# Strassen's seven products for the second matrix of a mixture-of-experts layer, one product after the other, with a transposed result

## The chip, the core and the metric

The kernel runs on one core of one Trainium2 chip. The metric is the device time of one execution in microseconds. The core has a matrix engine (TensorE, PE in the profile; its weight loads are PEld), a vector engine (VectorE, DVE), a scalar engine (ScalarE, ACT), GpSimd (POOL) and a queue (SyncE, SP) from which every DMA of this kernel is issued. Matmuls write into PSUM, which has eight banks of 128 partitions x 512 fp32 columns.

## The reference

Attention without a softmax feeds two MLPs ("MoE" layers with one expert) in a row, all in fp32. 4608 tokens, model width 512, hidden width 2048:

```python
kv = np.einsum('bhsd,bhse->bhde', k, v)
out = np.einsum('bhsd,bhde->bhse', q, kv)
x = out / np.sqrt(np.mean(out * out, axis=-1, keepdims=True) + 1e-06) * g_norm
...
h = x @ w_in                       # first MoE
g = s * np.maximum(h, 0.0) ** 2 + b
x = g @ w_out
h = x @ w_in2                      # second MoE
g = h * (1.0 / (1.0 + np.exp(-1.702 * h)))
return g @ w_out2
```

The weights arrive as 64-bit numbers, seen in the kernel as pairs of 32-bit words.

## The kernel before, in words

**Precision.** Every fp32 operand is split into a high part (rounded to the matmul's float32r) and a low part (the rest). One product of two 128-wide pieces is three matmuls: high x high, high x low, low x high. ScalarE makes high parts (a copy), VectorE low parts (a subtraction).

**Tiling.** The tokens are nine blocks of 512 (`T`), the hidden width 16 tiles of 128 (`NF`), the model width four tiles of 128 (`NP`). Activations are kept transposed (features on partitions, tokens on columns). A first product of a block (`mlp_h`, line 405) is 12 matmuls of 512 columns per hidden tile, a second product (`mlp_o`, 443) 12 matmuls per hidden tile into four PSUM banks that are accumulated over all 16 hidden tiles. In the first MoE the weights of the second product are the stationary operand and the result stays transposed; in the second MoE the activations are stationary, and the result comes out with tokens on partitions, as the output wants it.

**Plain blocks and pairs.** Three blocks of the first MoE (`NPLAIN`) and the last block of the second run plainly (`plain`, 599). All others run as pairs of blocks (`strassen`, 615): three pairs in the first MoE, four in the second. In a pair the first product is done by Strassen's method in Winograd's form: with the operands cut into quarters, seven products (`PRODUCTS`, line 41) take the place of eight. `g1_product` (484) does one of the seven for two hidden tiles, 6 matmuls; `g1_sum` (518) adds the seven results into the four quarters, on VectorE out of PSUM; product 4 adds onto product 0's bank, product 6 onto product 3's. `g1_act` (542) applies the activation. The second product of a pair is the ordinary one: for each hidden tile f and each of the two blocks, 12 matmuls (`mlp_o`), whose operands `g2_hi` (565) and `g2_lo` (569) prepare from the activated tile `R[f]`, and whose weights `wo_load` (179) reads back from DRAM, 512 KB each.

**Operands.** The seven operands of the token side (`x_operands`, 640, with `x_load`, `x_sub`, `x_hi`, `x_lo`) are made during the second product of the pair before, those of the weight side are made once (`s_sums`, `op_hi`, `op_lo`, `op_store`, 198 to 226), kept in DRAM (`wsd`) and loaded for each pair (`op_load`, 233). The second MoE's weights are prepared while the first MoE's pairs run (the loop at 751): those of the first product as eight operands, those of the second as a high and a low half (`w_hi`, 159; `w_lo`, 163; `wo_store`, 173).

**Order.** Nothing is scheduled by a planner: every step is entered with a slot by `at(slot, function, ...)` (581), the entries are sorted by slot, and the instructions are emitted in that order. Each engine and the SP queue run their instructions in this order, and waits come from the data and the buffers. A slot is 12 matmuls of 512 columns; a pair's first stage has 28 slots (half a slot per product), its second stage 32. A load is entered `LEAD` = 4 slots ahead of its use, `g2_hi` 2.5 and `g2_lo` 2.0 slots ahead:

```python
at(base + 2 * f - LEAD, wo_load, m, f)
...
slot = base + 2 * f + n
at(slot, mlp_o, m, j + n, f)
...
at(slot - 2.5, g2_hi, m, j + n, f, n)
at(slot - 2.0, g2_lo, m, j + n, f, n)
```

SBUF buffers are 42 large ones (two tiles of 512 columns, `new4`) and 22 small ones (`new2`), reused in the order in which they were given back; so are the eight PSUM banks. The attention of later blocks (`attention`, 595) runs as small units within the first stages of the first MoE's first two pairs: a product, a square on ScalarE, a high and low part, two matmuls for the mean (`att_mean`, 335), then a root and a correction.

Of the kernel before, what the change touches and what calls it, by code (L numbers as in the profile page):

```python
# [60 lines left out]
def kernel(ctx: ExitStack, tc: tile.TileContext, qT, kv_h, kvt, cst,  # L61
# [111 lines left out]
    def wo_store(m, f):  # L173
        w = W[m, f, 1]
        nc.sync.dma_start(out=wod[m][f], in_=w.bitcast(F32))
        if m:
            drop(W.pop((m, f, 1)))

    def wo_load(m, f):
        w = W[m, f, 1] = new4(F32R, "w")  # L180
        nc.sync.dma_start(out=w.bitcast(F32), in_=wod[m][f])

    def a_store(f):
        w = W[0, f, 0]
        for c, name in enumerate((("A11", "A12"), ("A21", "A22"))[f % 2]):
            nc.sync.dma_start(
                out=wsd[0][f // 2][:, OPS.index(name), :].rearrange("p (h c) -> p h c", h=2),
                in_=w[:, :, c * 256:(c + 1) * 256].bitcast(F32),
            )
# [8 lines left out]
    def s_sums(m, i):  # L198
        a, a2 = (vals[m, 2 * i + n, 0].bitcast(F32) for n in range(2))
        s12, s34 = sums[m, i] = new2(F32, "s12"), new2(F32, "s34")  # L200
        lo, hi = slice(0, 256), slice(256, 512)
        dve.tensor_add(out=s12[:, lo], in0=a2[:, lo], in1=a2[:, hi])
        dve.tensor_sub(out=s34[:, lo], in0=a[:, lo], in1=a2[:, lo])
        dve.tensor_sub(out=s12[:, hi], in0=s12[:, lo], in1=a[:, lo])
        dve.tensor_sub(out=s34[:, hi], in0=a[:, hi], in1=s12[:, hi])

    def op_source(m, i, k):
        return vals[m, 2 * i + k, 0] if k < 2 else sums[m, i][k - 2]

    def op_hi(m, i, k):  # L210
        src = op_source(m, i, k).bitcast(F32)
        t = parts[m, i, k] = new4(F32R, "op")
        act.activation(t[:, :, 0:256], src.rearrange("p (a c) -> p a c", a=2), AF.Copy)

    def op_lo(m, i, k):
        src = op_source(m, i, k)
        t = parts[m, i, k]
# [4 lines left out]
    def op_store(m, i, k):  # L222
        t = parts.pop((m, i, k))
        for a, name in enumerate((("A11", "A12"), ("A21", "A22"), ("S1", "S2"), ("S3", "S4"))[k]):
            nc.sync.dma_start(out=wsd[m][i][:, OPS.index(name), :], in_=t[:, a, :].bitcast(F32))
        drop(t)

    def op_done(m, i):
        drop(*sums.pop((m, i)), *(vals.pop((m, 2 * i + n, 0)) for n in range(2)))
# [8 lines left out]
    def wi_load(m, f):  # L238
        t = W[m, f, 0] = new4(F32R, "w")
        for a, name in enumerate((("A11", "A12"), ("A21", "A22"))[f % 2]):  # L240
            nc.sync.dma_start(out=t[:, a, :].bitcast(F32), in_=wsd[m][f // 2][:, OPS.index(name), :])

    def wi_part(m, f, h, c):
        w = W[m, f, 0]
# [160 lines left out]
    def mlp_h(m, j, f):  # L405
# [3 lines left out]
        for c in range(NP):  # L409
            wh, wlo = (wi_part(m, f, i, c) for i in range(2))  # L410
# [32 lines left out]
    def mlp_o(m, j, f):  # L443
        gh, gl = G.pop((m, j, f))
        w = W[m, f, 1]
        wh, wlo = w[:, 0, :], w[:, 1, :]
        if f == 0:
            acc[m, j] = [psum("o") for c in range(NP)]
        for c in range(NP):
            o = acc[m, j][c]  # L450
            cc = slice(c * P, (c + 1) * P)
# [4 lines left out]
            for n, (a, x) in enumerate(pairs):  # L456
                pe.matmul(o, lhsT=a, rhs=x, start=(f == 0 and n == 0), stop=(f == NF - 1 and n == 2))  # L457
# [5 lines left out]
    def mlp_store(m, j):  # L463
# [9 lines left out]
        for c, t in enumerate(staged):  # L473
            if m == 0:
                nc.sync.dma_start(out=xd[1][j][c], in_=t)
                done.add((1, j, c))
            else:
                nc.sync.dma_start(out=out[j * T + c * P:j * T + (c + 1) * P, :], in_=t)
            drop(t)
# [4 lines left out]
    def g1_product(m, i, k):  # L484
# [5 lines left out]
        if first:  # L490
            st[k] = psum("abcdefg"[k])
        else:
            st[k] = st[0] if k == 4 else st[3]
# [14 lines left out]
    def relu2(m, r, src=None):  # L508
        if m == 0:
            act.activation(r, r if src is None else src, AF.Relu)  # L510
        else:
            src = r if src is None else src
            t = new2(F32, "t")
            act.activation(t, src, AF.Sigmoid, scale=1.702)
            dve.tensor_mul(out=r, in0=src, in1=t)
            drop(t)

    def g1_sum(m, i, k):
        f, f2 = 2 * i, 2 * i + 1
# [11 lines left out]
        elif k == 3:  # L531
            R[f2] = new4(F32, "r")
            dve.tensor_add(out=R[f2][:, 1, :], in0=st[3], in1=st["u3"])  # L533
        elif k == 5:
            dve.tensor_add(out=R[f2][:, 0, :], in0=st[5], in1=st["u3"])
            drop(st.pop(5), st.pop("u3"))
        elif k == 6:
            dve.tensor_add(out=R[f][:, 1, :], in0=st[6], in1=st["u2"])
            drop(st.pop(6), st.pop("u2"))
            del st[3]  # L540

    def g1_act(m, i, k):
        f, f2 = 2 * i, 2 * i + 1
        if k == 4:
            R[f] = new4(F32, "r")
            relu2(m, R[f][:, 0, :], st[4])
            drop(st.pop(4))
            del st[0]
        elif k == 3 and m == 1:
            relu2(m, R[f2][:, 1, :])  # L550
        elif k == 5:
            if m == 0:
                relu2(m, R[f2])
                act.activation(R[f2], R[f2], AF.Square)
            else:
                relu2(m, R[f2][:, 0, :])
        elif k == 6:
            relu2(m, R[f][:, 1, :])
            if m == 0:
                act.activation(R[f], R[f], AF.Square)  # L560

    def g2_scale(m, f):
        act.activation(R[f], R[f], AF.Identity, scale=s_col, bias=b_col)

    def g2_hi(m, j, f, n):
        gh, gl = G[m, j, f] = new2(F32R, "gh"), new2(F32R, "gl")
        act.activation(gh, R[f][:, n, :], AF.Copy)  # L567

    def g2_lo(m, j, f, n):
        gh, gl = G[m, j, f]  # L570
        dve.tensor_sub(out=gl, in0=R[f][:, n, :], in1=gh.bitcast(F32))  # L571
        if n:
            drop(R.pop(f))
# [41 lines left out]
    def strassen(m, j, base, shift):  # L615
# [8 lines left out]
        base += 28 + shift  # L624
        for f in range(NF):
            at(base + 2 * f - LEAD, wo_load, m, f)
            for n in range(2):
                slot = base + 2 * f + n
                at(slot, mlp_o, m, j + n, f)
                if n == 0 and m == 0:  # L630
                    at(slot - 3.3, g2_scale, m, f)
                at(slot - 2.5, g2_hi, m, j + n, f, n)
                at(slot - 2.0, g2_lo, m, j + n, f, n)
                if n:
                    at(slot, wo_done, m, f)
        at(base + 31.1, mlp_store, m, j)
        at(base + 32.1, mlp_store, m, j + 1)
        return base

    def x_operands(m, j, base, step):  # L640
        a1, a2, b1, b2 = (m, j, 0), (m, j, 1), (m, j + 1, 0), (m, j + 1, 1)
# [14 lines left out]
        at(base + step * 11, x_done, m, (b1, a1))  # L656

# [24 lines left out]
    seconds = {0: [], 1: []}  # L682
    starts = {0: [], 1: []}
    for j in range(NPLAIN, NB, 2):
        starts[0].append(base)
        seconds[0].append(strassen(0, j, base, j == NPLAIN))
        base = seconds[0][-1] + 32
    half = base
    for j in range(0, NB - 1, 2):
        starts[1].append(base)  # L690
        seconds[1].append(strassen(1, j, base, 0))
        base += 60
# [17 lines left out]
    for n, j in enumerate(range(NPLAIN + 2, NB, 2)):  # L710
        attend(units(j, j + 1), starts[0][n] + 0.4, 3.1, (0, 0.7, 1.3, 1.8, 2.3, 3.2, 5.5))


    for n, j in enumerate(range(NPLAIN, NB, 2)):
        if n == 0:
            x_operands(0, j, 32 * NPLAIN - 14, 1.25)
        else:
            x_operands(0, j, seconds[0][n - 1] + 5, 2.3)
    for n, j in enumerate(range(0, NB - 1, 2)):
        x_operands(1, j, (seconds[1][n - 1] if n else seconds[0][-1]) + 5, 2.3)  # L720
# [5 lines left out]
    for k in range(2):  # L726
        slot = seconds[1][-1] + 10 + 4 * k
# [7 lines left out]
    for f in range(NF):  # L735
        at(34 + 3 * f, a_store, f)
        at(35 + 3.5 * f, wo_store, 0, f)
    for i in range(NF // 2):
# [3 lines left out]
        at(slot + 1.5, s_sums, 0, i)  # L742
        for k in (2, 3):
            at(slot + k, op_hi, 0, i, k)
            at(slot + k + 1, op_lo, 0, i, k)
            at(slot + k + 3, op_store, 0, i, k)
        at(slot + 4, op_done, 0, i)
# [3 lines left out]
    for i in range(NF // 2):  # L751
        for n in range(2):
            u = (1, 2 * i + n, 0)
            at(slot - 4, w_load, *u)
            at(slot + n, w_low, *u)
            at(slot + n + 1, w_top, *u)
            at(slot + n + 1.5, w_sum, *u)
        at(slot + 3.5, s_sums, 1, i)
        for k in range(4):
            at(slot + 3 + 1.2 * k, op_hi, 1, i, k)  # L760
            at(slot + 4 + 1.2 * k, op_lo, 1, i, k)
            at(slot + 6 + 1.2 * k, op_store, 1, i, k)
# [57 lines left out]
```

## Time and profile before

| | |
|---|---|
| median of 3 runs | 1649.23 us (1647.7 to 1649.74) |
| the profiled execution's own time | 1650.12 us |
| its span, first to last instruction | 1648.3 us |
| TensorE (PE) busy | 1614.7 us, 98% |
| VectorE (DVE) busy | 944.6 us, 57% |
| ScalarE (ACT) busy | 810.7 us, 49% |
| DMA | 334.51 MB, mean 203 GB/s |

The profile is one execution. Busy times are sums over the whole span; a stage can look quite different from the mean, so the stages have to be cut out: the first MoE's pairs take from about 390 us to 904.7, the second MoE's four pairs from 904.7 to 1557.5 (a first stage of 76.2 us and a second of 87.0 us each), and the last plain block the rest. Instructions are named by line, engine, operation and tiles, written out<-in.

### The profile page before, as it was taken

To read this page: it belongs to the slowest core of one execution; us is meant where nothing else is said; L and a number is where in the kernel's file an instruction comes from. 1 tells how busy PE (TensorE), PEld (TensorE's weight loads), DVE (VectorE), ACT (ScalarE), POOL (GpSimd) and SP (SyncE) were. 2 spreads that over 40 slices of the span, in tenths; PEclk is the share of its full clock that TensorE was granted. 3 is DMA by queue.
4 is the path that set the end of the run, shared out by engine and by line. 5 is a ranking of instruction groups with operands and counts; after the bars stand their busy time and mean duration, and the time that the engine had idled before them with its cause. 6 is when DMAs were issued, how large, how long until landed. Compare 5 with 4: busy or idle time off the path is not lost.

```text
span 1648.3 us, 19714 instructions
## 1 busy us (share of the span) xinstructions
PE 1614.7 (98%) x7124; PEld 1317.5 (80%) x7124; DVE 944.6 (57%) x1485; ACT 810.7 (49%) x1273; POOL 18.3 (1%) x22
## 2 busy tenths in 40 slices
PE   7989999899999999999999999999999999999999
PEld 5766777788878877888888888888888888888887
DVE  6888346666778477845661675267426742672122
ACT  5766456656897389845872343124312431242122
POOL 1000000000000000000000000000000000000000
PEclk9999999999999999999999999999999999999999
DMA  7963645657977696849851852186227612760280
GB/s 244 287 192 99 209 157 182 218 204 261 335 259 256 218 371 237 285 165 372 280 213 39 325 203 98 55 309 216 85 71 293 230 71 85 284 233 32 97 324 26
DMA packets 150386, 334.51 MB, mean 203 GB/s; under 512 B 22801, under 2 KB 55569, under 8 KB 150289
## 3 DMA queue, kind: packets, MB, share of 16 engines
q1 hardware_dynamic: 150288, 333.24, 57.7%
q8 instruction: 57, 0.93, 0.2%
q14 instruction: 41, 0.33, 0.1%
HBM read 256.77 MB, written 76.41 MB: 202 GB/s over the span
## 4 chain that ended last, share of the span: by engine, by line
PE 61%; DVE 0%; issue 0%; DVEq 0%
PE o L457 34%; PE d L500 7%; PE a L500 7%; PE f L500 3%; PE c L500 3%; PE b L500 3%; PE h L413 3%; DVE st L468 0%; DVE sl L331 0%; PE ms L339 0%; DVE op L218 0%; DVE r L533 0%; DVEq L218 0%
## 5 line engine op out<-in xcount | busy, mean ns | idle before, releaser
L457 PE MATMUL o<-gh,w 128*128 128x512 f32 x1152 | 366.2, 392 | 0.3
L457 PE MATMUL o<-w,gh 128*128 128x512 f32 x1152 | 354.6, 389 | 0.0
L457 PEld LDWEIGHTS o<-gh,w 128*128 128x128 f32 x1152 | 217.1, 188 | 47.1 <-ACT gh L436 2.0
L457 PEld LDWEIGHTS o<-w,gh 128*128 128x128 f32 x1152 | 216.2, 188 | 44.9
L571 DVE TENSOR_TENSOR gl<-r,gh 128x512 fp32r<-128x512 f32 x224 | 150.9, 688 | 163.3 <-ACT gh L567 160.8
L457 PE MATMUL o<-gl,w 128*128 128x512 f32 x576 | 226.3, 393 | 10.5 <-DVE gl L440 10.3
L457 PE MATMUL o<-w,gl 128*128 128x512 f32 x576 | 224.1, 389 | 0.0
L567 ACT ACTIVATE gh<-r 128x512 fp32r<-128x512 f32 x224 | 136.6, 625 | 161.8 <-PE o L457 159.6
L413 PE MATMUL h<-xh,w 128*128 128x512 f32 x512 | 177.8, 408 | 0.2 <-DVE xh L374 0.2
L500 PE MATMUL d<-xh,wl 128*128 128x512 f32 x448 | 157.1, 391 | 1.2 <-DVE r L533 1.2
L500 PE MATMUL a<-xh,wl 128*128 128x512 f32 x448 | 157.3, 392 | 0.0
L457 PEld LDWEIGHTS o<-gl,w 128*128 128x128 f32 x576 | 108.5, 188 | 37.8 <-DVE gl L440 15.1
L457 PEld LDWEIGHTS o<-w,gl 128*128 128x128 f32 x576 | 108.1, 188 | 22.5
L468 DVE COPY st<-o 128x512 f32<-128x512 f32 x36 | 24.7, 690 | 167.9 <-PE o L457 167.8
L413 PEld LDWEIGHTS h<-xh,w 128*128 128x128 f32 x512 | 97.7, 191 | 24.5 <-issue 1.0
L470 ACT ACTIVATE st<-o 128x512 f32<-128x512 f32 x36 | 21.2, 596 | 175.7 <-PE o L457 175.7
L413 PE MATMUL h<-xl,w 128*128 128x512 f32 x256 | 101.7, 397 | 1.9 <-POOL xl L375 1.9
L500 PEld LDWEIGHTS d<-xh,wl 128*128 128x128 f32 x448 | 84.1, 188 | 19.2 <-DVE r L533 1.6
L500 PEld LDWEIGHTS a<-xh,wl 128*128 128x128 f32 x448 | 84.1, 188 | 17.9 <-issue 0.5
L522 ACT ACTIVATE c<-a 128x512 f32<-128x512 f32 x56 | 33.4, 596 | 120.8 <-PE a L500 120.8
L500 PE MATMUL a<-xl,wl 128*128 128x512 f32 x224 | 87.2, 389 | 0.0
L500 PE MATMUL d<-xl,wl 128*128 128x512 f32 x224 | 87.2, 389 | 0.0
(100 smaller groups left out, 2412.7 us busy)
## 6 DMA issues: line engine op xcount, KB each, us to landing
wl<-wsd SPq DMA_DIRECT2D x168, 512.0 KB, 7.3
w<-wod SPq DMA_DIRECT2D x128, 512.0 KB, 6.2
wsd<-op SPq DMA_DIRECT2D x96, 256.0 KB, 3.5
raw<-in_w_in SPq DMA_DIRECT2D x32, 512.0 KB, 6.6
kv_in<-in_kv SPq DMA_DIRECT2D x32, 512.0 KB, 4.9
raw<-in_w_out SPq DMA_DIRECT2D x32, 512.0 KB, 6.5
wod<-w SPq DMA_DIRECT2D x32, 512.0 KB, 3.6
wl<-wsd SPq DMA_DIRECT2D x56, 256.0 KB, 6.6
```

The lines of the kernel that those rows point to most:

```text
L413: pe.matmul(h, lhsT=a, rhs=b, start=(n == 0), stop=(n == 3 * NP - 1))
L457: pe.matmul(o, lhsT=a, rhs=x, start=(f == 0 and n == 0), stop=(f == NF - 1 and n == 2))
L468: dve.tensor_copy(out=t, in_=o)
L470: act.activation(t, o, AF.Copy)
L500: pe.matmul(o, lhsT=a, rhs=b, start=(first and n == 0), stop=(n == 5), skip_group_check=not first)
L522: act.activation(st["c1"], st[0], AF.Copy)
L567: act.activation(gh, R[f][:, n, :], AF.Copy)
L571: dve.tensor_sub(out=gl, in0=R[f][:, n, :], in1=gh.bitcast(F32))
```

## The change

The second product of the second MoE's four pairs becomes a Strassen product too. Its inner dimension is the hidden width, so the hidden tiles are cut into an upper and a lower half: the activated tiles are now kept by quarter ("11", "12", "21", "22"), four double tiles each (`r_half`). The seven products run one after the other (`second_products`): product k is four steps n of 12 matmuls (`g2_product`), which accumulate over the hidden tiles in two PSUM banks, and after its fourth step `g2_sum` adds the result to what came before, or stages a quarter of the output, which `g2_store` writes. The operands on the activation side are made within the stage: `t_sums` makes T2 in place of the quarter "12" during the first stage, `go_sum` makes T3, T1 and T4 (products 2, 3 and 5), `go_hi` and `go_lo` split each operand. The weights of w_out2 are prepared as eight operands (`s_sums`, `op_hi`, `op_lo`, `op_store` with `which` = 1), kept in `wo2` and loaded for each step (`go_load`, 512 KB). The stage has 28 slots instead of 32.

The weights are now the stationary operand everywhere, so the second MoE's result comes out transposed: the output tensor is (512, 4608), and the host turns it round (its `.T` after the run lies outside the device time). The last plain block uses the same order of operands.

The next pair's operand sums T1 to T4 are made by `x_sums` in the first stage and put into DRAM; `x_splits` loads all seven in the second stage and splits them. In the first MoE's pairs the activation of the quarters is done for two groups at a time (`r_act`), and `g2_scale` works on quarters.

```diff
-    wod = [[dp.tile([P, 2, 512], F32, name=f"wod{m}_{f}") for f in range(NF)] for m in range(2)]
+    wod = [dp.tile([P, 2, 512], F32, name=f"wod{f}") for f in range(NF)]
+    wo2 = [dp.tile([P, NF // 2, 512], F32, name=f"wo2{name}") for name in OPS]
...
     def wo_load(m, f):
         w = W[m, f, 1] = new4(F32R, "w")
-        nc.sync.dma_start(out=w.bitcast(F32), in_=wod[m][f])
+        if m == 0:
+            nc.sync.dma_start(out=w.bitcast(F32), in_=wod[f])
+        else:
+            for a, name in enumerate(OP_PAIRS[1][f % 2]):
+                nc.sync.dma_start(out=w[:, a, :].bitcast(F32), in_=op_place(m, f // 2, 1, name))
...
     def mlp_o(m, j, f):
...
-            if m == 0:
-                pairs = ((wh[:, cc], gh), (wh[:, cc], gl), (wlo[:, cc], gh))
-            else:
-                pairs = ((gh[:, cc], wh), (gh[:, cc], wlo), (gl[:, cc], wh))
...
+            wh, wlo = (w_part(m, f, 1, h, c) for h in range(2))
+            for n, (a, x) in enumerate(((wh, gh), (wh, gl), (wlo, gh))):
+                pe.matmul(acc[m, j][c], lhsT=a, rhs=x, start=(f == 0 and n == 0), stop=(f == NF - 1 and n == 2))
...
+    def t_sums(n):
+        t = new4(F32, "t1")
+        dve.tensor_sub(out=t, in0=R["12", n], in1=R["11", n])
+        dve.tensor_sub(out=R["12", n], in0=R["22", n], in1=t)
+        drop(t)
+
+    TERMS = {"B11": "11", "T2": "12", "T3": ("12", "11"), "T1": ("22", "12"), "B21": "21", "T4": ("21", "12"), "B22": "22"}
...
+    def go_sum(k, n):
+        t = TERMS[PRODUCTS[k][1]]
+        if isinstance(t, tuple):
+            a, b = t
+            g = GOP[k, n] = new4(F32, "t")
+            dve.tensor_sub(out=g, in0=R[a, n], in1=R[b, n])
...
+    def go_hi(k, n):
+        src = GOP[k, n]
+        hi, lo = new4(F32R, "gh"), new4(F32R, "gl")
+        act.activation(hi, src, AF.Copy)
+        GOP[k, n] = src, hi, lo
+
+    def go_lo(k, n):
+        src, hi, lo = GOP[k, n]
+        dve.tensor_sub(out=lo, in0=src, in1=hi.bitcast(F32))
...
+    def go_load(k, n):
+        t = wl["o", k, n] = new4(F32R, "wl")
+        nc.sync.dma_start(out=t.bitcast(F32), in_=wo2[OPS.index(PRODUCTS[k][0])][:, 2 * n:2 * n + 2, :])
+
+    def g2_product(k, n):
+        w, x = wl.pop(("o", k, n)), GOP.pop((k, n))
+        first = k not in (4, 6)
+        for d in range(2):
+            if n == 0:
+                so[k, d] = psum("o") if first else so[0 if k == 4 else 3, d]
+            for i in range(2):
+                wh, wlo = (w[:, i, h * 256 + d * P:h * 256 + (d + 1) * P] for h in range(2))
+                xh, xl = (t[:, i, :] for t in x)
+                for e, (a, b) in enumerate(((wh, xh), (wh, xl), (wlo, xh))):
+                    pe.matmul(so[k, d], lhsT=a, rhs=b, start=(first and n == 0 and i == 0 and e == 0),
+                              stop=(n == 3 and i == 1 and e == 2), skip_group_check=not first)
+        drop(w, *x)
...
+    def g2_store(j, k, d):
+        n, half = {3: (1, 2), 4: (0, 0), 5: (0, 2), 6: (1, 0)}[k]
+        o_store(1, j + n, half + d, so.pop(("st", k, d)))
...
+            if i % 2 and m == 0:
+                for n, (q, fn) in enumerate((("22", AF.Relu), ("21", AF.Relu), ("22", AF.Square), ("21", AF.Square),
+                                             ("12", AF.Relu), ("11", AF.Square), ("12", AF.Square))):
+                    at(slot + 1.4 + 0.45 * n, r_act, q, i // 2, fn)
+            elif i % 2:
+                at(slot + 3.1, t_sums, i // 2)
...
+                if f % 4 < 2:
+                    at(slot - 3.3, g2_scale, *quarter(f, n)[:2])
...
+    def second_products(j, base):
+        for k in range(len(PRODUCTS)):
+            for n in range(4):
+                slot = base + 4 * k + n
+                at(slot, g2_product, k, n)
+                at(slot - LEAD, go_load, k, n)
+                at(slot - 3.2, go_sum, k, n)
+                at(slot - 2.4, go_hi, k, n)
+                at(slot - 1.7, go_lo, k, n)
+            for d in range(2):
+                at(slot + 0.6 + 0.5 * d, g2_sum, j, k, d)
+                if k > 2:
+                    at(slot + 2.6, g2_store, j, k, d)
+        return base + 28
...
+        for n, (name, *rest) in enumerate((("T3", "T3", b2, b1), ("T1", b1, b1, a1), ("T2", a1, b2, b1), ("T4", a2, a2, a1))):
+            at(base + step * n, x_sub, *rest)
+            at(base + step * n + 1.5, xs_store, j, name, rest[0])
...
+        for n, (name, key) in enumerate((("B11", a1), ("T2", "T2"), ("T3", "T3"), ("T1", "T1"), ("B21", a2), ("T4", "T4"), ("B22", b2))):
+            slot = base + step * n
+            at(slot - 3.5, *((x_load, *key) if name[0] == "B" else (xs_load, j, name)))
+            at(slot, x_hi, key, (1, name))
+            at(slot + 0.8, x_lo, key, (1, name), 1)
...
+    for j in range(0, NB - 3, 2):
+        x_sums(j + 2, firsts[1, j] + 4, 2)
+        x_splits(j + 2, seconds[1, j] + 5, 3.1)
...
     for i in range(NF // 2):
...
-        slot += 9
-        for n in range(2):
-            u = (1, 2 * i + n, 1)
-            at(slot - 4, w_load, *u)
-            for d, fn in ((0, w_low), (1, w_top), (1.5, w_sum), (2.5, w_hi), (3.5, w_lo)):
-                at(slot + d, fn, *u)
-            at(slot + 5.5, wo_store, 1, 2 * i + n)
-            slot += 5
+        for which in range(2):
...
+            at(slot + 3.5, s_sums, 1, i, which)
+            for k in range(4):
+                at(slot + 3 + 1.2 * k, op_hi, 1, i, which, k)
+                at(slot + 4 + 1.2 * k, op_lo, 1, i, which, k)
+                at(slot + 6 + 1.2 * k, op_store, 1, i, which, k)
+            at(slot + 7.7, op_done, 1, i, which)
+            slot += 9.5
...
-    args.append(nc.dram_tensor("out_0", (B * S, DM), F32, kind="ExternalOutput").ap())
+    args.append(nc.dram_tensor("out_0", (DM, B * S), F32, kind="ExternalOutput").ap())
...
-    return r.results[0]["out_0"]
+    return np.ascontiguousarray(r.results[0]["out_0"].T)
```

## Rows read from the trace of the kernel before

**Rows 1.** The page's first part: busy time, share of the span, instructions.

```profile
PE 1614.7 (98%) x7124; PEld 1317.5 (80%) x7124; DVE 944.6 (57%) x1485; ACT 810.7 (49%) x1273; POOL 18.3 (1%) x22
```

**Rows 2.** Busy time by stretch; first the columns, then stages of both MoEs.

```profile
core 0: us, PE busy (x) PEld busy (x) DVE busy (x) ACT busy (x) POOL busy (x), PEclk, DMA share, GB/s
...
414.00:491.00 77.00, 75.85 (x334) 61.53 (x333) 57.45 (x96) 69.10 (x101) 0.00 (x0) 1.00 0.83 293
...
578.00:654.50 76.50, 75.30 (x323) 59.90 (x322) 59.68 (x97) 66.19 (x99) 0.00 (x0) 1.00 0.84 305
...
741.50:817.70 76.20, 76.20 (x338) 63.10 (x337) 48.07 (x81) 49.34 (x70) 0.00 (x0) 1.00 0.92 334
...
1144.10:1231.10 87.00, 87.00 (x385) 72.03 (x385) 36.05 (x47) 26.41 (x41) 0.00 (x0) 1.00 0.26 96
1231.10:1307.30 76.20, 76.20 (x338) 63.10 (x337) 47.33 (x72) 23.60 (x45) 0.00 (x0) 1.00 0.71 249
```

**Rows 3.** The chain that ended last: start us, us, what.

```profile
654.48 87.04 PE o L457 x384
...
809.52 1.36 PE b L500 x6
...
1307.28 87.04 PE o L457 x384
```

**Rows 4.** Who waited for whom, TensorE, 272 to 700 us: total, times, longest.

```profile
PE ms L339 <- DVE sl L331: 8.0, 5, 2.9
PE d L500 <- DVE r L533: 1.2, 1, 1.2
```

**Rows 5.** Groups by line and form, VectorE and ScalarE.

```profile
L393 DVE TENSOR_TENSOR xl<-x,xh 128x1024 fp32r<-128x1024 f32 x51 | 62.1, 1218 | 0.0
L525 DVE TENSOR_TENSOR u<-b,c 128x512 f32<-128x512 f32 x56 | 38.6, 690 | 70.8 <-PE b L500 49.3 <-ACT t L514 13.7 <-ACT c L522 4.5
L400 DVE TENSOR_TENSOR x<-x 128x1024 f32<-128x1024 f32 x28 | 34.1, 1218 | 0.0
L218 DVE TENSOR_TENSOR op<-s,op 128x512 fp32r<-128x512 f32 x32 | 21.6, 683 | 1.1 <-ACT op L213 1.1
L202 DVE TENSOR_TENSOR s<-ca 128x256 f32<-128x256 f32 x16 | 6.7, 417 | 0.1
...
L389 ACT ACTIVATE xh<-x 128x1024 fp32r<-128x1024 f32 x51 | 53.2, 1045 | 0.0
L470 ACT ACTIVATE st<-o 128x512 f32<-128x512 f32 x36 | 21.2, 596 | 175.7 <-PE o L457 175.7
L213 ACT ACTIVATE op<-s 128x512 fp32r<-128x512 f32 x32 | 19.7, 620 | 8.3 <-DVE s L204 8.3
```

**Rows 6.** VectorE in order of time, start of a second stage: start us, us, instruction, idle before.

```profile
983.93 3.09 DVE L571 TENSOR_TENSOR gl<-r,gh 128x512 fp32r<-128x512 f32 x5
986.94 1.22 DVE L393 TENSOR_TENSOR xl<-x,xh 128x1024 fp32r<-128x1024 f32 x1
988.08 0.68 DVE L571 TENSOR_TENSOR gl<-r,gh 128x512 fp32r<-128x512 f32 x1
...
995.02 0.69 DVE L571 TENSOR_TENSOR gl<-r,gh 128x512 fp32r<-128x512 f32 x1 [0.97 <-ACT gh L567]
...
1000.46 0.69 DVE L571 TENSOR_TENSOR gl<-r,gh 128x512 fp32r<-128x512 f32 x1 [2.03 <-ACT gh L567]
```

**Rows 7.** DMA issues on the page: KB each, median us from issue to landing.

```profile
wl<-wsd SPq DMA_DIRECT2D x168, 512.0 KB, 7.3
...
raw<-in_w_in SPq DMA_DIRECT2D x32, 512.0 KB, 6.6
...
raw<-in_w_out SPq DMA_DIRECT2D x32, 512.0 KB, 6.5
```

More of the change, by code (lines that the diff above doesn't have):

```diff
@@ L220, in op_lo, with op_store, op_done @@
         )
[L222 to L225, printed above, removed]
+    def op_store(m, i, which, k):
+        t = parts.pop((m, i, which, k))
+        for a, name in enumerate(OP_PAIRS[which][k]):
+            nc.sync.dma_start(out=op_place(m, i, which, name), in_=t[:, a, :].bitcast(F32))
         drop(t)
-    def op_done(m, i):
-        drop(*sums.pop((m, i)), *(vals.pop((m, 2 * i + n, 0)) for n in range(2)))
+    def op_done(m, i, which):
+        drop(*sums.pop((m, i, which)), *(vals.pop((m, 2 * i + n, which)) for n in range(2)))
     wl = {}
@@ L239, in wi_load, with w_part @@
         t = W[m, f, 0] = new4(F32R, "w")
[L240 to L244, printed above, removed]
+        for a, name in enumerate(OP_PAIRS[0][f % 2]):
+            nc.sync.dma_start(out=t[:, a, :].bitcast(F32), in_=op_place(m, f // 2, 0, name))
+    def w_part(m, f, which, h, c):
+        w = W[m, f, which]
         if m == 0:
@@ L473, in mlp_store, with o_store @@
         for c, t in enumerate(staged):
[L474 to L479, printed above, removed]
+            o_store(m, j, c, t)
+    def o_store(m, j, c, t):
+        if m == 0:
+            nc.sync.dma_start(out=xd[1][j][c], in_=t)
+            done.add((1, j, c))
+        else:
+            nc.sync.dma_start(out=out[c * P:(c + 1) * P, j * T:(j + 1) * T], in_=t)
+        drop(t)
     st, R = {}, {}
@@ L506, in g1_product, with r_half @@
                 drop(*xop.pop((m, name)))
[L508 to L516, printed above, removed]
+    def r_half(q, i):
+        if i % 2 == 0:
+            R[q, i // 2] = new4(F32, "r")
+        return R[q, i // 2][:, i % 2, :]
     def g1_sum(m, i, k):
-        f, f2 = 2 * i, 2 * i + 1
         if k == 0:
@@ L539, in g1_sum, with gate @@
             drop(st.pop(6), st.pop("u2"))
             del st[3]
+    def gate(r, h):
+        t = new2(F32, "t")
+        act.activation(t, h, AF.Sigmoid, scale=1.702)
+        dve.tensor_mul(out=r, in0=h, in1=t)
+        drop(t)
     def g1_act(m, i, k):
-        f, f2 = 2 * i, 2 * i + 1
         if k == 4:
-            R[f] = new4(F32, "r")
-            relu2(m, R[f][:, 0, :], st[4])
+            r = r_half("11", i)
+            if m == 0:
+                act.activation(r, st[4], AF.Relu)
+            else:
+                gate(r, st[4])
@@ L547, in g1_act @@
             drop(st.pop(4))
             del st[0]
[L549 to L563, printed above, removed]
+        elif m == 1 and k in (3, 5, 6):
+            r = R[{3: "22", 5: "21", 6: "12"}[k], i // 2][:, i % 2, :]
+            gate(r, r)
@@ new lines, in g2_sum @@
+    def g2_sum(j, k, d):
+        o = so[k, d]
+        if k == 0:
+            c1 = so["c1", d] = new2(F32, "c1")
+            act.activation(c1, o, AF.Copy)
+        elif k == 1:
+            u2 = so["u2", d] = new2(F32, "u2")
+            dve.tensor_add(out=u2, in0=o, in1=so["c1", d])
+            drop(o, so.pop(("c1", d)))
+        elif k == 2:
+            u3 = so["u3", d] = new2(F32, "u3")
+            dve.tensor_add(out=u3, in0=o, in1=so["u2", d])
+            drop(o)
+        else:
+            t = new2(F32, "st")
+            if k == 4:
+                act.activation(t, o, AF.Copy)
+            else:
+                dve.tensor_add(out=t, in0=o, in1=so["u2" if k == 6 else "u3", d])
+            if k != 3:
+                drop(o)
+            if k > 4:
+                drop(so.pop(("u3" if k == 5 else "u2", d)))
+            so["st", k, d] = t
@@ L726 @@
     for k in range(2):
[L727 removed]
+        slot = seconds[1, NB - 3] + 10 + 4 * k
         key = (1, NB - 1, k)
```

197 lines of the change are left out of this document (108 added, 89 removed).

## The prediction

> **What bounds the kernel now.** I read the profile from the outside in. The page's first part says that TensorE is busy for 98% of the span and that VectorE, ScalarE and the DMA queue have room as averages [rows 1]. An average hides stages, so the next view is the table by stretches, cut at the kernel's own stages [rows 2]. In the pair stages of the second MoE TensorE is busy for every microsecond: 87.00 of 87.00 us in a second-product stage, 76.20 of 76.20 in a first-product stage, at a granted clock of 1.00 (the 2.4 GHz level), while VectorE works 36.05 us of 87 there. The chain of waits says the same in time order: 384 second-product matmuls follow each other in 87.04 us, and six first products take 1.36 us [rows 3], both 0.2267 us per matmul. So the matmul count sets the time of these stages at 0.2267 us apiece, and an engine beside TensorE matters only if it becomes late. Earlier it is less even: in the first MoE's pairs TensorE waits here and there, mostly for VectorE's part of an attention unit (8.0 us in five waits from 272 to 700 us, and 1.2 us at one first product) [rows 4].
>
> **What is removed.** For a pair of 512-token blocks the second product takes 16 (hidden tiles) x 2 (blocks) x 12 = 384 matmuls. The new second_products runs 7 products x 4 steps x 12 = 336. That is 48 fewer per pair, 192 over the four pairs of the second MoE; every matmul keeps its 512 columns and its own weight load. At the rows' 0.2267 us this is 192 x 0.2267 = **43.5 us**, all on the path that sets the end, since TensorE has no gap in these stages to absorb it. Beside it a page of the Trainium skill, TensorE: Matmul & The Clock Gate (section Back-to-back issue gap), gives about 131 ns per matmul as the sustained pace at 512 columns: by that the removal would be worth about 25 us (an estimate from that page). The trace disagrees by its own count, 87.04 us over 384, so the sum keeps 0.2267.
>
> **What is added in the second MoE's second stage, per pair.** Call the time of 12 matmuls a slot, 2.72 us; the stage becomes 28 slots, 76.2 us. VectorE gets 28 low parts of 1024 columns, 12 operand sums of 1024, 10 sums out of PSUM of 512, and 7 low parts of the next pair's operands. By the durations of such instructions, 1.22 us and 0.69 us [rows 5], that is 47 x 1.22 + 10 x 0.69 = 64 us of 76.2, where it had 36 of 87. ScalarE gets 28 + 7 copies of 1024 at 1.05 us and 4 of 512 at 0.60, some 39 us. Neither is the bound as an average. The dense stretch is where products 2 and 3 (T3, T1), both made by a subtraction, come one behind the other. I walk VectorE's queue there. It cannot run ahead of the sum over product 1, which TensorE finishes in its first half at 7.5 slots, 20.4 us into the stage. From there to the low part of product 3's third step it has 12 instructions of 1024 and 4 of 512. Back to back they start 1.14 us and 0.60 us apart, since one overlaps the end of the one before it [rows 6]: 12 x 1.14 + 4 x 0.60 = 16.1 us, done at 36.5. TensorE wants that tile one matmul after 14 slots, at 38.3. The margin is 1.8 us; with the full durations and no overlap it is 12 x 1.22 + 4 x 0.69 = 17.4, done at 37.8, and 0.5 us are left. Product 4 needs no sum, so VectorE recovers, and product 5, between two products without sums, never comes as close. Cost taken: 0, with an upper end in the first rival.
>
> **First stage of these pairs.** t_sums puts 8 subtractions of 1024 into it and x_sums 4 more (three pairs), 12 x 1.22 = 14.6 us over the 47 us that VectorE has there [rows 2]: 62 of 76.2. The place that counts is the sum over product 3: product 6 adds onto the same PSUM bank, one slot after product 3 has ended, and may not start before that sum has read it. t_sums is placed 0.6 slot behind the sum, so it delays what follows, 2.3 us, against 3.5 slots between two such sums: no cost.
>
> **DMA.** Operands now come as 28 loads of 512 KB per stage instead of 16, with 7 loads of the next operands, 8 output stores of 256 KB and the first loads of the next stage: about 22.6 MB in 76.2 us, 296 GB/s, where the stage had 96. The last first stage of the first MoE moves 334 GB/s at a share of 0.92 with TensorE busy throughout [rows 2], so this fits. A load takes a median 7.3 us from issue to landing [rows 7] and is queued 4 slots, 10.9 us, ahead. All go through SP's queue in order, so behind a store that waits for VectorE the loads stand too: each output store stands at least 1.5 slots behind its sum's place, and SP reaches it after the data are there. The transposed output is written in rows of the same 2 KB, now 18 KB apart; the nearest rows are input loads of 512 KB, from strided rows (w_in) 6.6 us and from a contiguous block (w_out) 6.5 [rows 7], so I take nothing for it, and the last four stores of the kernel keep their size. The last block keeps its matmuls with weights and activations exchanged, as the first MoE has them already, whose 384 take 87.04 us too [rows 3].
>
> **The first MoE.** There the matmuls stay the same, but while its pairs run, the second MoE's output weights are prepared as eight operands instead of two halves: 16 more copies on ScalarE (0.62 us, 10 us in all), 16 more subtractions (0.68) and 32 sums of 256 columns (0.42) on VectorE, 24 us in all [rows 5], and 8 MB more stores, spread over about 420 us. The activation of the hidden quarters is also gathered, 7 operations of 1024 columns behind every second group instead of some behind every group; their sum is the same within 2%. ScalarE has 69 of 77 us busy in the first such stage and 66 of 76.5 in the second [rows 2]; both also carry attention units, whose mean waits for ScalarE and VectorE. So some waits will grow. Below: the present 9.2 us in this stretch [rows 4] could shrink with the new order, by 2 us at most, since that is about what lies inside the two crowded stages. Above: they double, 9 us. I take **+2 us**, near the low end, because VectorE adds only 24 us over 420 and ScalarE 10.
>
> **Sum.** The profiled execution took 1650.12 us, its span 1648.3 and 1.8 around it, 0.9 above the median of the three runs, 1649.23. 1650.12 - 43.5 + 2 = 1608.6; against the median, 1607.7.
>
> **Rivals.**
> *VectorE is late in the second stage.* The 0.5 to 1.8 us margin is less than what VectorE already idles for a ScalarE copy in front of one low part, 1.0 to 2.0 us [rows 6]; two such handovers in the dense stretch use it up. For: an operand now passes VectorE, ScalarE and VectorE again. Against: the copies are queued 0.7 slot ahead, and behind a backlog they are done before VectorE comes. Price: 1 to 4 us in each of four pairs, 1612 to 1624.
> *The first MoE's crowded stages get slower.* For: ScalarE is at 87 to 90% there, and seven activations come in one row. Against: today's two waits cost 2.4 us in both stages. Price 5 to 9 us over the present, 1611 to 1615.
> *Slower than before: SP's queue holds the weight loads.* For product 3 to 6 the output stores stand among the loads of the next product. If a sum is late by more than the 1.5 slots (4.1 us) before its store and the 3.6 us between lead (10.9) and landing (7.3), 8 us in all, the four loads behind land late, and TensorE waits at each of 4 x 4 = 16 places. More than 43.5 / 16 = 2.7 us at each, a sum late by about 11 us, makes the kernel slower; at a full landing of 7.3 us per place it would be 1607.7 + 117 = 1725. Against: the walk has no lateness near 8 us.
> The change cannot fail to remove the matmuls; the loops fix their number.
>
> **How the numbers follow.** Forecast 0.72 (1604 to 1611), VectorE late 0.12, first MoE crowded 0.12, SP's queue 0.03, and 0.01 for a gain that is eaten up just to nothing. The low end, 1604, is no added wait and the faster end of the runs shown (1.5 below the median); the high end, 1619, takes in the crowded first MoE and most of the late VectorE. A measurement of this kernel tells 0.2%, 3.3 us, from no change; faster by more than that: 0.96, within: 0.01, slower: 0.03.
>
> **What would show it.** In the profile after, the page should count 6932 matmuls (7124 less 192), and each second stage should be 76.2 us with TensorE busy throughout, in pieces of 2.72 us per product step, VectorE busy about 64 us. A wait of a second product for a low part on VectorE, around product 3, shows the first rival; growth of the mean's waits beyond 9 us before 700 us the second; waits of second products for weight loads the third. A stage of more than 78 us, or matmuls 0.2267 us apart no longer, makes the forecast wrong.

## The result, and the profile after

The kernel with the change takes 1605.85 us (median of 4 runs, 1604.21 to 1606.35), the kernel before 1649.49 in the same comparison: a ratio of 0.9736, 95% interval 0.9719 to 0.9752, 43.6 us less. The forecast was 1607.7.

The profiled execution is the fastest of the four, 1604.21 us with a span of 1602.4. The page's first part, to be held against [rows 1]:

```profile
PE 1568.8 (98%) x6932; PEld 1280.1 (80%) x6932; DVE 1114.2 (70%) x1621; ACT 846.3 (53%) x1261; POOL 18.9 (1%) x22
```

There are 192 matmuls fewer, as the loops say, and TensorE is still at 98%. VectorE has 170 us more work in a shorter span, ScalarE 36, and none of it has become time.

The table by stretches, cut at the new stages, against [rows 2] (the second, fourth and sixth line are second-product stages):

```profile
core 0: us, PE busy (x) PEld busy (x) DVE busy (x) ACT busy (x) POOL busy (x), PEclk, DMA share, GB/s
902.10:978.10 76.00, 76.00 (x337) 62.97 (x336) 58.41 (x81) 25.12 (x42) 0.00 (x0) 1.00 0.72 266
978.20:1054.30 76.10, 76.10 (x337) 63.04 (x336) 62.07 (x60) 34.91 (x38) 0.00 (x0) 1.00 0.82 284
1054.40:1130.40 76.00, 76.00 (x337) 62.96 (x336) 58.43 (x81) 23.83 (x41) 0.00 (x0) 1.00 0.65 234
1130.50:1206.60 76.10, 76.10 (x337) 63.03 (x337) 62.17 (x60) 34.92 (x38) 0.00 (x0) 1.00 0.80 280
...
738.70:814.90 76.20, 76.20 (x338) 63.12 (x337) 50.70 (x90) 47.28 (x68) 0.00 (x0) 1.00 0.96 349
814.90:902.00 87.10, 87.10 (x386) 72.16 (x385) 40.23 (x56) 48.64 (x64) 0.00 (x0) 1.00 0.38 142
```

TensorE is busy for every microsecond of the second MoE's stages, at a granted clock of 1.00, now beside a VectorE that works 62 of 76 us (36 of 87 before) and a DMA share of 0.8 (0.26 before). The chain of waits gives the borders, to be held against [rows 3]: the first matmul of the second MoE, two of its second stages, and the first matmuls of the last plain block.

```profile
902.00 1.36 PE a L504 x6
...
1130.48 76.16 PE o L632 x336
...
1435.12 76.16 PE o L632 x336
1511.28 5.44 PE h L424 x24
```

A second stage is 336 matmuls in 76.16 us, 0.2267 us each as before. The four pairs take 1511.28 - 902.00 = 609.28 us. Before, with 4 x (76.16 + 87.04), they took 652.80. The difference is 43.52 us, 192 x 0.2267 to the digit.

The span fell by 45.9. The remaining 2.4 come from before the first MoE's pairs, from code whose work the change leaves as it was: the first Strassen product starts at 383.4 us in this profile and at 386.0 in the one before. In the eleven profiles of the changed kernel and of its variants below it starts between 383.4 and 387.2, so this is the spread of a run and not the change. From there to the second MoE the two kernels take 518.6 and 518.7 us. The matmuls of the last plain block, whose operands are exchanged, take 87.37 us from the first to the end of the last, against 87.09 before: 0.3 us more, which the prediction put at nothing.

What TensorE waited for between 272 and 700 us, against [rows 4]; from 700 us to the end no matmul of the pairs has a wait in this view:

```profile
PE ms L350 <- DVE sl L342: 7.7, 6, 2.9
PE a L504 <- ACT c L520: 0.7, 1, 0.7
PE d L504 <- DVE r L530: 0.3, 1, 0.3
```

8.7 us where it was 9.2: the wait for ScalarE is new, the one for VectorE at a first product is smaller.

The walk along VectorE's queue can be checked instruction by instruction. VectorE in order of time in the stage that begins at 1130.48, from the first sum over product 1 to the low part of product 3's third step (the first of the last line's two):

```profile
1150.92 0.69 DVE L643 TENSOR_TENSOR u<-o,c 128x512 f32<-128x512 f32 x1
1151.53 1.22 DVE L597 TENSOR_TENSOR t<-r 128x1024 f32<-128x1024 f32 x1
1152.66 0.69 DVE L643 TENSOR_TENSOR u<-o,c 128x512 f32<-128x512 f32 x1
...
1162.34 0.69 DVE L647 TENSOR_TENSOR u<-o,u 128x512 f32<-128x512 f32 x1
1162.94 1.22 DVE L597 TENSOR_TENSOR t<-r 128x1024 f32<-128x1024 f32 x1
1164.08 1.22 DVE L404 TENSOR_TENSOR xl<-x,xh 128x1024 fp32r<-128x1024 f32 x1
1165.21 0.69 DVE L647 TENSOR_TENSOR u<-o,u 128x512 f32<-128x512 f32 x1
1165.81 2.36 DVE L611 TENSOR_TENSOR gl<-t,gh 128x1024 fp32r<-128x1024 f32 x2
```

The sum starts 20.44 us into the stage (walk: 20.4), the low part starts at 1165.81 and is done 1.22 later, 36.55 us in (walk: 36.5). TensorE asks for it one matmul after 14 slots, at 1130.48 + 38.3 = 1168.8. The margin of 1.8 us is there; in the other three pairs it is 1.6, 1.8 and 2.3. Every other low part of this stage is done at least 2.7 us before its matmul, so this tile is the nearest to being late.

### The profile page after: what moved, and what is told of

Same layout as the page of the kernel before. It is cut to its first block, busy times and chain, and to the rows that moved or that the text cites. A ratio compares the mean times of both kernels' runs of the same rounds, so it can differ in the third digit from the quotient of the medians.

```text
span 1602.4 us, 19757 instructions
## 1 busy us (share of the span) xinstructions
PE 1568.8 (98%) x6932; PEld 1280.1 (80%) x6932; DVE 1114.2 (70%) x1621; ACT 846.3 (53%) x1261; POOL 18.9 (1%) x22
## 4 chain that ended last, share of the span: by engine, by line
PE 60%; DVE 0%; issue 0%
PE o L632 19%; PE o L461 14%; PE d L504 7%; PE a L504 7%; PE b L504 3%; PE f L504 3%; PE c L504 3%; PE h L424 3%; DVE st L472 0%; DVE r L530 0%; DVE sl L342 0%; PE ms L350 0%; DVE op L229 0%
## 5 line engine op out<-in xcount | busy, mean ns | idle before, releaser
L461 PE MATMUL o<-gh,w 128*128 128x512 f32 x1280 | 407.5, 391 | 0.3
L632 PE MATMUL o<-gh,wl 128*128 128x512 f32 x896 | 276.7, 389 | 0.0
L461 PE MATMUL o<-gl,w 128*128 128x512 f32 x640 | 251.0, 392 | 10.5 <-DVE gl L451 10.3
L632 PEld LDWEIGHTS o<-gh,wl 128*128 128x128 f32 x896 | 168.2, 188 | 34.9
L632 PE MATMUL o<-gl,wl 128*128 128x512 f32 x448 | 174.5, 389 | 0.0
L632 PEld LDWEIGHTS o<-gl,wl 128*128 128x128 f32 x448 | 84.1, 188 | 17.4
L575 DVE TENSOR_TENSOR gl<-r,gh 128x512 fp32r<-128x512 f32 x96 | 65.1, 688 | 38.8 <-ACT gh L570 36.8
L606 ACT ACTIVATE gh<-t 128x1024 fp32r<-128x1024 f32 x48 | 51.0, 1062 | 72.4 <-DVE t L597 62.3
L559 ACT ACTIVATE r<-r 128x1024 f32<-128x1024 f32 x84 | 84.8, 1047 | 0.0
L611 DVE TENSOR_TENSOR gl<-r,gh 128x1024 fp32r<-128x1024 f32 x64 | 77.2, 1219 | 7.2 <-ACT gh L606 7.2
```

The source lines that it names most:

```text
L461: pe.matmul(acc[m, j][c], lhsT=a, rhs=x, start=(f == 0 and n == 0), stop=(f == NF - 1 and n == 2))
L559: act.activation(R[q, n], R[q, n], fn)
L575: dve.tensor_sub(out=gl, in0=R[q, i][:, half, :], in1=gh.bitcast(F32))
L606: act.activation(hi, src, AF.Copy)
L611: dve.tensor_sub(out=lo, in0=src, in1=hi.bitcast(F32))
L632: pe.matmul(so[k, d], lhsT=a, rhs=b, start=(first and n == 0 and i == 0 and e == 0), stop=(n == 3 and i == 1 and e == 2), skip_group_check ...
```

## The experiments

The theory that goes into them: the gain is the removed matmuls at their pace, and everything else that the change adds is hidden, closest at product 3's third step. The rivals: other parts of the change gain or cost too; VectorE's sum of work counts, not one stretch; the weight loads are near their limit. All kernels below start from the changed one.

**Eight products instead of seven (e1).** In `g2_product`, for product 0, after its own matmuls:

```diff
+        if k == 0:
+            for d in range(2):
+                if n == 0:
+                    so["again", d] = psum("o")
+                for i in range(2):
...
+                        pe.matmul(so["again", d], lhsT=a, rhs=b, start=(n == 0 and i == 0 and e == 0),
+                                  stop=(n == 3 and i == 1 and e == 2))
+                if n == 3:
+                    drop(so.pop(("again", d)))
```

> Product 0 of each second-stage is issued a second time, into two spare PSUM banks that nobody reads: 48 more matmuls per pair, 192 in all, so the stage has the 384 matmuls that the ordinary product had; all else of the change stays. Theory (the gain is the matmul count at 0.2267 us, the rest of the change costs and gains nothing): 1605.85 + 192 x 0.2267 = 1649.4, within 2 us of the kernel before. Rival 1 (the new order of loads, quarters and operand sums itself gains, since the first MoE came out 2.6 us earlier): 1645 to 1647, clearly below the kernel before. Rival 2 (the change costs something that the shorter stages hide): above 1651.

Measured: 1650.05 us against 1650.02 for the kernel before, ratio 1.0004 (0.9995 to 1.0013). The chain of waits of this kernel, the last second stage of the first MoE and the first matmuls of the last block:

```profile
817.31 87.04 PE o L461 x384
1557.15 5.44 PE h L424 x24
```

From 817.31 + 87.04 = 904.35 to 1557.15 are 652.80 us, exactly what the four pairs took before the change. With the matmuls back, the whole gain is gone, and nothing more than the gain: the new operands, loads, stores and the transposed result neither cost nor gain anything that the run can tell (about 0.1%). Both rivals fall.

**Four low parts twice, in the dense stretch (e2) and at product 6 (e3).**

```diff
-        dve.tensor_sub(out=lo, in0=src, in1=hi.bitcast(F32))
+        for _ in range(2 if (k, n) in ((2, 2), (2, 3), (3, 0), (3, 1)) else 1):
+            dve.tensor_sub(out=lo, in0=src, in1=hi.bitcast(F32))
```

In e3 the list is the four steps of product 6.

> Four low parts of the dense stretch (product 2 steps 2 and 3, product 3 steps 0 and 1) are computed twice: 4 x 1.14 = 4.6 us more VectorE work per pair where the walk left a margin of 1.8 us. Theory (the margin is real, and it is this tile, product 3's third step, that comes late): a stall of 4.6 - 1.8 = 2.8 us in each of four pairs, 11 us in all, about 1617, and the second-products' wait for a low part on VectorE shows in the waits, largest at that step or spread over the three before it. Rival (VectorE has slack to spare in the stage, 14 of 76 us, so it absorbs 4.6): 1606, no change. Rival (VectorE is already the pace, all of it counts): 1605.85 + 18 = 1624.

> The same extra VectorE work, 4 x 1.14 us per pair, on the four low parts of product 6, where VectorE idles 2.3 and 5.4 us for TensorE. Theory (only the dense stretch is near its limit): 1606, no change within 0.1%. Rival (VectorE's sum of work over the stage counts): 1617 to 1624 like the dense one.

Measured: 1619.09 us for e2 (ratio to the kernel before 0.981, 0.9796 to 0.9825) and 1606.01 for e3 (0.9732, 0.9718 to 0.9747). The same work costs 13 us in one place and nothing in the other (e3's four pairs take 609.28 us, as in the changed kernel). One stage each, in the table by stretches, first e2's and then e3's:

```profile
980.90:1060.60 79.70, 77.17 (x337) 62.57 (x336) 66.93 (x65) 34.79 (x38) 0.00 (x0) 1.00 0.80 271
```

```profile
1283.80:1359.90 76.10, 76.10 (x337) 63.06 (x336) 66.93 (x64) 34.88 (x38) 0.00 (x0) 1.00 0.81 279
```

VectorE is busy for 66.93 us in both; the mean says nothing about which of the two is late. In e2's order of time on VectorE the low parts of product 3 are, in the stage that begins at 980.97:

```profile
1012.07 2.48 DVE L612 TENSOR_TENSOR gl<-t,gh 128x1024 fp32r<-128x1024 f32 x2
...
1015.59 2.48 DVE L612 TENSOR_TENSOR gl<-t,gh 128x1024 fp32r<-128x1024 f32 x2
...
1021.46 2.35 DVE L612 TENSOR_TENSOR gl<-t,gh 128x1024 fp32r<-128x1024 f32 x2
```

and TensorE's waits there, in its own order of time:

```profile
1014.59 0.50 PE L633 MATMUL o<-gl,wl 128*128 128x512 f32 x1 [0.47 <-DVE gl L612]
1018.12 0.50 PE L633 MATMUL o<-gl,wl 128*128 128x512 f32 x1 [0.52 <-DVE gl L612]
1022.72 0.51 PE L633 MATMUL o<-gl,wl 128*128 128x512 f32 x1 [1.54 <-DVE gl L612]
```

The third step's low part starts 1021.46 - 980.97 = 40.5 us into the stage, 5.2 later than in the changed kernel (35.3). Take off the margin of 1.8, and 3.4 us a pair are left; the four pairs take 1527.66 - 904.81 = 622.85 us, 13.6 more, 3.4 each. The expected 2.8 was small because a low part repeated on the same tile costs 1.25 to 1.3 us and not 1.14 (2.48 for two, where two on different tiles take 2.36).

**Loads entered later: 2 slots ahead (e4) and 0.2 (e7).** In `second_products`:

```diff
-                at(slot - LEAD, go_load, k, n)
+                at(slot - 2, go_load, k, n)
```

> The weight loads of the second stage are entered 2 slots ahead of their use (5.4 us) instead of 4 (10.9). The loads land 5.2 to 6.1 us after their issue in the median, 13 at most. Theory (loads go out when their place in SP's queue comes, and the 10.9 us lead is what covers the landing): about half the 112 loads come 0.3 to 2 us late, TensorE waits for weight loads by 20 to 80 us in all, 1626 to 1686, and the time of a stall is not made good. Rival (SP runs ahead of its slots when buffers are free, so the entered slot hardly matters): 1606 to 1610.

> The weight loads are entered only 0.2 slots ahead of their use; with 2 slots nothing changed. Theory (SP runs some 2 to 3 slots, 5 to 8 us, ahead of the entered slots as long as no store holds it, against 5 to 6 us from issue to landing): the cover is now used up, loads that stand behind an output store come late, waits of a few us at products 3 to 6, 1610 to 1640. Rival (buffers alone decide when a load goes out, and the slot never matters): 1606 to 1608 again.

Measured: 1607.41 us for e4 (0.974, 0.9724 to 0.9757), no change, and 1622.68 for e7 (0.9832, 0.9815 to 0.9848), inside its theory's range. In e4 the rival was right: its four pairs take 609.28 us, to the digit what they take in the changed kernel. The SP queue's loads in e4's stage that begins at 1133.23:

```profile
1133.26 0.32 SPq L620 DMA_DIRECT2D wl<-wo2A  x1
1134.11 1.65 SPq L620 DMA_DIRECT2D wl<-wo2S  x3
1136.51 7.95 SPq L620 DMA_DIRECT2D wl<-wo2S  x3
```

The first line is product 0's last step (used at slot 3), the second product 1's first three (slots 4 to 6), issued by 1135.8, so they go out 3 to 5 slots ahead, although they are entered 2 ahead. SP runs ahead of the slots as far as buffers and stores let it. In the changed kernel itself, the queue's three longest waits in the second MoE:

```profile
SPq L620 <- PE o L632: 102.7, 45, 4.9
SPq L620 <- PE f L504: 62.0, 8, 7.8
SPq L485 <- DVE st L654: 60.2, 23, 7.2
```

SP waits for free buffers (lines 1 and 2) and at the output stores for VectorE's sums (line 3), 23 times; what is queued behind them still lands in time. An example from the changed kernel's stage that begins at 1130.48, the first two output stores and the loads behind them:

```profile
1173.40 1.78 SPq L485 DMA_DIRECT2D out<-st  x2
1176.76 0.80 SPq L620 DMA_DIRECT2D wl<-wo2A  x2
```

The two loads are those of product 5's last two steps. They are entered four slots ahead, but the first is issued at 1176.76 for slot 22, which begins at 1190.3: 13.6 us or five slots ahead, where such loads land in a median 4.8 us.

With 0.2 slots the cover is gone. The profiled run of e7, the slowest of its four (1625.96 us), takes 629.3 us for the four pairs, 20.0 more than the changed kernel, 5 a pair. The second products' waits, TensorE, in the second MoE:

```profile
PE o L632 <- DMA wl<-wo2S: 4.7, 5, 1.5
PE o L632 <- DMA wl<-wo2A: 4.6, 6, 1.4
PE o L632 <- ACT gh L606: 4.0, 2, 2.0
```

The chain that ended last shows what the lead had covered. Pieces of it in e7's stage that begins at 979.41: a staged sum on VectorE, the output store that waited for it, the weight load behind that store, and the second products that waited for the load.

```profile
1022.97 0.70 DVE st L654
...
1023.68 0.34 SPq L485
...
1024.12 4.45 DMA wl<-wo2A
...
1028.70 4.36 PE o L632 x18
```

The same sequence comes once more in this stage, from 1049.22. Not all of the loss is the lead: the chain also goes through late high parts on ScalarE, the buffers are handed out in another order, and SP stands 90.0 us in five waits for the buffer of a temporary of `t_sums` (7.5 in three in the changed kernel). How much of the 17 us between the medians each share has was not separated.

**Contiguous stores (e5) and the operand sums back in the second stage (e6).** e5 writes each result tile to `out[j * T + c * P:j * T + (c + 1) * P, :]`, with the output tensor shaped (4608, 512) again, so that its result is in neither kernel's order. e6:

```diff
-        x_sums(j + 2, firsts[1, j] + 4, 2)
-        x_splits(j + 2, seconds[1, j] + 5, 3.1)
+        x_operands(1, j + 2, seconds[1, j] + 5, 2.0)
```

> The result tiles of the second MoE are written to a contiguous stretch of 256 KB each instead of 2 KB rows that lie 18 KB apart; the output is therefore not put in the reference's order (it is a tile-wise transposed one). Theory (the strided store costs nothing, no instruction waits for it): 1606, the same within 0.2%. Rival (strided rows slow the stores, and with them the loads behind): 2 us or more faster than with the transposed layout.

> The next pair's operand sums are made in the second stage again (four subtractions of 1024 more on VectorE there, in three pairs, one of them more in the dense stretch than the walk had), without the round trip of T1 to T4 through DRAM. Theory (only the 1.8 us margin of the dense stretch counts): about 1.1 to 2.3 us more work ahead of product 3's third step, so a stall of 0 to 0.6 us in each of three pairs, 1606 to 1608. Rival (the move of the sums into the first stage is part of the gain): more than 1610. Rival (the round trip through DRAM costs): below 1604.

Measured: 1607.58 us for e5 (0.9746, 0.9731 to 0.9761) and 1605.19 for e6 (0.9735, 0.9721 to 0.975). Neither differs from the changed kernel: their four pairs take 609.28 and 609.27 us. Storing the transposed rows costs nothing against storing contiguous tiles; what a result in the reference's own order would cost on the device, no run here shows. Nor were the sums' move to the first stage and their round trip through DRAM needed: with 66 of 76 us busy, VectorE in e6 still brings the low part of product 3's third step in time, but not by much. In its stage that begins at 1131.62, the first sum over product 1 and that low part (the first of the two):

```profile
1153.32 0.69 DVE L643 TENSOR_TENSOR u<-o,c 128x512 f32<-128x512 f32 x1
...
1168.19 2.37 DVE L611 TENSOR_TENSOR gl<-t,gh 128x1024 fp32r<-128x1024 f32 x2
```

One of the subtractions stands ahead of the sum, which starts 21.7 us into the stage instead of 20.4. The low part is done at 1168.19 + 1.23 = 1169.42, 37.8 us in, and TensorE asks for it at 38.3. Of the margin of 1.8 us 0.5 are left (0.8 in the other two pairs), as the theory expected from about one subtraction more.

**Further: the first MoE's last pair (e8, e9).** If a removed matmul is worth 0.2267 us wherever VectorE can follow, the same product-by-product form should give 48 x 0.2267 = 10.9 us for a pair of the first MoE. e8 keeps its output weights as eight operands too and runs its last pair with the new stage; the main lines:

```diff
-        base = second_plain(j, seconds[0, j])
+        base = second_products(0, j, seconds[0, j]) if j == NB - 2 else second_plain(j, seconds[0, j])
...
+    for i in range(NF // 2):
+        slot = seconds[0, NPLAIN + 2 * (i % 2)] + 4 * i
+        at(slot + 0.2, w_join, 2 * i, 1)
+        at(slot + 2.2, w_join, 2 * i + 1, 1)
+        at(slot + 3, s_sums, 0, i, 1)
...
-            slot += 9.5
+            slot += 9
```

with the activation and scaling of that pair's quarters ahead of `t_sums`. e9 is e8 with the following pair's sums in the first stage, another order of the activations, and a preparation step of 9.3.

> The second product of the first MoE's last pair is done by the seven products too (the operand sums of its weights are made from the tiles that the two pairs before have loaded anyway; the activation and scaling of its quarters are done ahead of the split). Theory (every removed matmul is worth 0.2267 us where VectorE can follow): 48 matmuls fewer, 10.9 us, 1595; VectorE gets 35 us in the two stages before, where it works 60 and 63 of 87 us, which may give back 0 to 4. Rival (ScalarE and VectorE are too full around the start of that stage, 12 activations of 1024 in three slots): the gain is given back in waits of second products there, 1600 to 1608.

> As e8, with its two losses mended: the operand sums of the following pair are made in the first stage (x_sums, x_splits) as in the second MoE, the activation and scaling of the last quarters is put in the order in which products 0 and 1 need them, the quarter 21 of the last two steps is activated within the second stage, and the preparation of the second MoE's weights runs at 9.3 instead of 9 slots per group. Theory (e8 gave back 4.6 us in its new stage because VectorE and ScalarE were late at products 0 to 3, and about 3 us in the stage of the pair before): most of these 7.6 us come back, 1596 to 1600. Rival (the first MoE's engines are full, the losses only move): 1602 to 1606.

> The changed kernel once more, unaltered, beside e9 on the same chip: 1604 to 1608. Theory (the part before the first pair's first product is the same work in both kernels, and its length varies from run to run by 2 to 3 us): its second-product stages take 87.04 and 76.16 us as before, and the first of its second stages starts anywhere from 476 to 479 us.

Measured: e8 1604.01 us (0.9724, 0.9709 to 0.9738), e9 1608.83 (0.9749, 0.9736 to 0.9762), the changed kernel beside e9 1606.47 (0.9739, 0.9726 to 0.9752). e8 and the changed kernel are not told apart by these intervals, and e9 is no better. In e8 the weight loads (PEld) of the new stage's second products wait for VectorE:

```profile
PEld o L632 <- DVE gl L611: 5.6, 8, 1.1
```

From the first Strassen product (386.3) to the second MoE (977.67 - 76.16 = 901.5) e8 takes 515.2 us against 518.5 in the changed kernel run beside e9 (386.4 to 904.9): 3.3 of the 10.9 us remain. Of the rest, 4.7 went in the new stage, which takes 80.8 us (820.7 to 901.5) instead of 76.16, and 3.5 in the first stage of the pair before (91.5 us against 88.0); the first pair's first stage is 0.6 shorter. e9 takes 521.0 us for the same stretch (387.2 to 908.3), 2.5 more than the changed kernel in spite of 48 matmuls fewer. Most of its waits are at other places, here the longest of TensorE's weight loads from 660 to 910 us:

```profile
PEld o L632 <- DVE gl L611: 2.7, 3, 1.1
PEld d L504 <- DVE r L530: 2.6, 1, 2.6
PEld c L504 <- DMA wl<-wsd: 2.6, 1, 2.6
PEld a L504 <- issue: 2.2, 1, 2.2
```

Neither theory held. In e8 the rival's range was met, but part of the loss lies ahead of the place that it named; e9 is slower than even its rival allowed. That the work prepared there for the second MoE leaves no room, so that what is taken from one queue comes back at another, fits these rows but is argued and not shown; nor was it separated which of e9's edits brought the new waits. The changed kernel run again beside e9 kept its time and its four pairs (609.28 us); the first of its second stages starts at 479.4 us, a little past the range expected.

## Why the prediction was right

**What is removed.** 43.5 us forecast, 43.52 between the borders of the stages, and e1 gives it back whole. The trace's pace of 0.2267 us decided. By the figure of the Trainium skill's page TensorE: Matmul & The Clock Gate (section Back-to-back issue gap) the gain would have been about 25 us (an estimate from that page); the measured 43.6 does not bear that out here.

**What is added in the second stage.** Cost 0 taken and found. The walk was right to 0.05 us in its end and named the tile that is nearest to being late; e2 shows that work ahead of it costs time beyond the margin, e3 that the same work elsewhere does not. VectorE was forecast at 64 us a stage and shows 62.1, ScalarE at 39 and shows 34.9: durations were added although neighbours overlap by about 0.1 us, and the first two or three of the 28 steps are already split in the first stage, so both sums are upper ends.

**First stage.** 62 us of VectorE forecast, 58.4 found, no wait.

**DMA.** The total was right (296 GB/s forecast, 280 found, share 0.8), no load is late, and the strided store costs nothing (e5). The working of it was wrong in one step: "SP reaches it after the data are there". SP reaches the output stores before the data are there and waits, 60.2 us in 23 waits for VectorE's sums and 17.1 in 8 for ScalarE's copies. The loads behind them are in time because SP runs further ahead than the four slots in which I put the cover: five slots in the rows above. That this term came out at nothing was luck as far as this step goes. The last block's exchange of operands was taken as nothing and cost 0.3 us.

**The first MoE.** "+2 us" was the term that was mis-sized: 518.6 us against 518.7, so 0. The added preparation and the gathered activation fit beside the matmuls, and TensorE's waits there did not grow (8.7 us against 9.2). Without that term the sum reads 1605.7.

**The rivals.** VectorE late in the second stage: its margin was as small as said, 1.8 us, and e2 shows the price once it is exceeded; it was not exceeded. The crowded first MoE did not come; e8 and e9 got little or nothing out of adding more to it. The queue of weight loads: the store waits of that rival are in the trace, without its lateness; with the lead taken away, in e7, the lateness is there too.

## What to carry to other kernels

Where the engine that sets the pace has no gap in a stage, the price of work taken from it is count times the start-to-start time in that stage, and the forecast is decided by whether anything beside it becomes late. For that, walk the queue of the fullest neighbour through its densest stretch, from an instruction that can't start early to the tile that is needed next, with start-to-start times and not with durations or the stage's mean: 66.93 us busy was harmless in e3 and cost 3.4 us a pair in e2. Place work that comes with a change in the slack behind the dense stretch; moving a load's slot does nothing as long as its buffers and the queue set its start (e4), and costs time once the lead is gone (e7).

## What was not expected of the hardware

Two VectorE instructions of 1024 columns on different tiles take 2.36 us together (start to start 1.14), two that write the same tile one after the other 2.48, as e2 shows. The second instruction on the same tile starts about 0.1 us later. In e2 the two also read the same tiles, so that it is the shared output that matters is not shown.
